# Moving three pieces of block-end work in a fused FFT and mixture-of-experts kernel

## The chip, the cores and the metric

The kernel runs on one core of one Trainium2 chip. The metric is the device time of one execution in microseconds (us). Engines are named TensorE (PE in the profile; its weight loads are PEld), VectorE (DVE), ScalarE (ACT), GpSimd (POOL) and SyncE (SP, which issues most DMAs).

## The reference

```python
X = np.fft.fft(np.fft.fft(x, axis=1), axis=2).real       # x: (8, 3072, 256), then (24576, 256) tokens
h = X @ w_in                                             # 256 -> 2048
x = (h * (1 / (1 + np.exp(-1.702 * h)))) @ w_out         # gelu by sigmoid, 2048 -> 256
# second layer, on tokens with x @ w_skip > 0; the others stay as they are
e_idx = np.argmax(x @ w_gate, axis=1)                    # 8 experts
y = gate_w * (np.maximum(x @ w1[e_idx], 0) @ w2[e_idx])  # 256 -> 1024 -> 256, weighted by the softmax
out = x + y
```

## The kernel before

Phase 1 (`Phase1`) does the transform and the first layer and sends each token's row to its expert's region in DRAM; phase 2 (`Phase2`) runs the experts. The change is in phase 1.

The sequence transform uses symmetries, so each of the 8 batches is two half-batches ("even" and "odd") of three blocks; a block makes 512 tokens. There are 48 blocks of 8 steps, 384 steps `g` in all, and the order of all instructions on each engine's queue is written out by hand. In a step:

- `hstep(g)`: twelve matmuls of 256 columns on TensorE (line 795), then on VectorE the sums `pp`, `h+`, `h-` (L799, L801, L802).
- `ystep(g - 2)`: the second product of the step before last, 24 matmuls of 264 columns (L826). It needs `gh`, and for its last third `gl`, of that step. The four results `y0` to `y3` collect in four PSUM banks over the 8 steps of a block.
- `gelu(g)`: two gelus on ScalarE (L809, L810), giving `gh` and the full value, and on GpSimd the difference `gl` (L811).
- At the end of a block, `finish`: `y0` and `y1` are copied to `rows` by VectorE, `y2` and `y3` by ScalarE (L832). The next block's product writes the same banks.
- Then the entries of `side` for this step.

`side` holds, among others: the routing of a block, one part a step: `a1` in the step behind the block's end (L836, then `route1`, L724 to L729, which ends in the one-hot matrix `oh`), `a2` (`route2`, sums over tokens on TensorE, L738 and L740), `a3` (`route3`, which adds the running base, L750 to L754), and four scatters of rows by GpSimd (L758). Further the transform of the next half-batch: `p0` runs one piece on TensorE (`piece_mm`, L252, nine matmuls), and in the next step's `side` it is evacuated by `evac_even` (L264 to L271) or `evac_odd0` and `evac_odd1` (L276 to L286). Last, in even half-batches and the first steps of odd ones, the folds of the next batch's input on VectorE (L205 to L237).

Pieces and routing sums share one PSUM bank, tag `misc`; whoever comes next waits until the last reader is done. The rows tiles are a pair of buffers (`rows`, bufs=2), which the mini tokens (8 tokens, one a batch) share. Left-over work of the loop's last blocks prepares phase 2.

Of the kernel before, what the change touches and what calls it, by code (L numbers as in the profile page):

```python
# [12 lines left out]
F32 = mybir.dt.float32  # L13
# [5 lines left out]
ALU = mybir.AluOpType  # L19
# [4 lines left out]
P = 128  # L24
# [12 lines left out]
NSTEP = NF // 2  # L37
RW = 266
NW = 264
BIG = float(1 << 20)  # L40
LAG = 2
# [115 lines left out]
class Phase1:  # L157
    def __init__(self, tc, ctx, nb, a, reg, k):
        self.tc, self.nc, self.nb, self.a, self.reg, self.k = tc, tc.nc, nb, a, reg, k
        self.ident, self.xs = k["ident"], k["xs"]  # L160
        self.side = defaultdict(list)
        self.pos = defaultdict(list)
        self.rts = {}
        self.scattered = False
        nc = self.nc
        cp = self.cp = ctx.enter_context(tc.tile_pool(name="cp", bufs=1))
        self.wch = cp.tile([P, 2, FF], F32R, name="wch")
        self.wcl = cp.tile([P, 2, FF], F32R, name="wcl")
        self.woh = cp.tile([P, NF, NW], F32R, name="woh")
        self.wol = cp.tile([P, NF, NW], F32R, name="wol")  # L170
        self.w128 = cp.tile([P, NF], F32, name="w128")
        self.coef = cp.tile([P, 2, CW], F32, name="coef")
        self.spec = cp.tile([P, 4, nb], F32, name="spec")
        self.mini = cp.tile([P, 8], F32, name="mini")
        self.tri = cp.tile([P, 2, P], BF16, name="tri")
        self.rid = cp.tile([P, 2, 4, 2], F32, name="rid")
        self.k8 = cp.tile([P, 4, 8], F32, name="k8")
        self.base = cp.tile([P, 8], F32, name="base")
        self.base0 = cp.tile([P, 8], F32, name="base0")
        dp = self.dp = ctx.enter_context(tc.tile_pool(name="dp", bufs=1, space=DRAM))  # L180
        self.yd = dp.tile([nb, 2, HC], F32, name="yd")
        self.ydm = dp.tile([nb, 1], F32, name="ydm")
        self.ps = ctx.enter_context(tc.tile_pool(name="ps", bufs=1, space=PSUM))
        self.left = ctx.enter_context(ExitStack())
        self.right = ctx.enter_context(ExitStack())
        self.yr = self.open(self.right, "yr", "right")
        self.fa = self.open(self.right, "fa", "right")
# [431 lines left out]
    def plan(self, hb):  # L619
        nc = self.nc  # L620
        b, odd = hb // 2, hb % 2
        g0 = hb * NBLK * NSTEP
        last = hb == 2 * self.nb - 1
        if last:
            return
        add = lambda s, f: self.side[g0 + s].append(f)
        le = nc.gpsimd
        st = {}
        if not odd:
# [8 lines left out]
            def p0(p):  # L638
                sh, sl = self.s
                q = self.piece_mm(st["cm"][4 + p % 2], sh, sl, p, KC)  # L640
                st["q"] = q
            def e0(p):
                st["xp"] = self.evac_odd0(b, p, st["q"])
            def e1(p):
                self.evac_odd1(p, st["xp"], st["q"], *st["y"], le)
            for p, s in enumerate((10, 13, 15, 21) if hb == 0 else (1, 4, 6, 7)):
                add(s, lambda p=p: p0(p))
                add(s + 1, (lambda p=p: e0(p)) if p % 2 == 0 else (lambda p=p: e1(p)))
            if b + 1 < self.nb:
                def ld(i):  # L650
                    st["r", i] = self.load_raw(b + 1, i // 2, i % 2)
# [36 lines left out]
        else:  # L688
# [16 lines left out]
                self.evac_even(b + 1, p, st["q"], *st["y"], le)  # L705
            for p, s in enumerate((17, 18, 20, 21) if b == 0 else (10, 13, 15, 18)):
                add(s, lambda p=p: p0(p))
                add(s + 1, lambda p=p: e0(p))
            def sp(c):
                if c == 0:  # L710
                    self.s = self.new_s()
# [28 lines left out]
            mm(ps[:, 8 * (i + 1) : n + 8], lhsT=self.tri[:, 1], rhs=o[:, : n - 8 * i], start=False, stop=i == nt - 1, skip_group_check=True)  # L740
        return ps

    def route3(self, rows, oh, ps, nt):
        nc, bp = self.nc, self.bp
        v = nc.vector
        q = bp.tile([P, 4, 8], F32, tag="rq", name="rq")
        m = bp.tile([P, 4], F32, tag="rm", name="rm")
        ix = bp.tile([P, 4], I32, tag="rix", bufs=2, name="rix")
        pv = ps[:, : nt * 8].rearrange("p (t e) -> p t e", t=nt)
        v.tensor_tensor(q[:, :nt], pv, self.base.unsqueeze(1).to_broadcast([P, nt, 8]), ALU.add)  # L750
        v.tensor_tensor(q[:, :nt], q[:, :nt], oh[:, :nt], ALU.mult)
        v.tensor_reduce(m[:, :nt], q[:, :nt], AX.X, ALU.add)
        v.tensor_scalar_add(ix[:, :nt], m[:, :nt], BIG)
        v.tensor_add(self.base, self.base, ps[:, nt * 8 : nt * 8 + 8])  # L754
        return ix

    def scatter(self, rows, ix, t):
# [14 lines left out]
    def main(self):  # L772
        nc, tc, nb = self.nc, self.tc, self.nb
        v = nc.vector
        ps = self.ps
# [6 lines left out]
        bp = self.bp  # L782
        if True:
# [30 lines left out]
            def ystep(g):  # L814
                gh, gl = gs.pop(g)
                s = g % NSTEP
                gb = g // NSTEP
                if s == 0:
                    ys[gb] = [ps.tile([P, NW], F32, tag=f"y{t}", name=f"py{t}") for t in range(4)]
                hi = [(gh, self.woh, 0), (gh, self.wol, 0), (gh, self.woh, 1), (gh, self.wol, 1)]  # L820
                lo = [(gl, self.woh, 0), (gl, self.woh, 1)]
                ends = s == NSTEP - 1
                for t, part in [(t, p_) for t in range(4) for p_ in (hi, lo)] if ends else [(t, p_) for p_ in (hi, lo) for t in range(4)]:
                    tk = slice(t * P, (t + 1) * P)
                    for n, (x_, w_, i) in enumerate(part):
                        nc.tensor.matmul(ys[gb][t], lhsT=x_[:, i, tk], rhs=w_[:, 2 * s + i], start=s == 0 and part is hi and n == 0, stop=ends and part is lo and n == 1)  # L826

            def finish(gb, gnow):
                st = {}
                rows = self.rp.tile([P, 4, RW], F32, tag="rows", bufs=2, name="rows")  # L830
                for t in range(4):
                    (v.tensor_copy if t < 2 else nc.scalar.copy)(rows[:, t, :NW], ys[gb][t])  # L832
                del ys[gb]

                def a1():
                    v.scalar_tensor_tensor(rows[:, :, NW:], self.rid[:, 1], float(gb * TB), self.rid[:, 0], ALU.mult, ALU.add)  # L836
                    st["oh"] = self.route1(rows, 4)
                    nc.sync.dma_start(self.a["out"][gb * TB : (gb + 1) * TB].rearrange("(t p) d -> p t d", p=P), rows[:, :, :D])

                def a2():  # L840
                    st["ps"] = self.route2(st["oh"], 4)

                def a3():
                    st["ix"] = self.route3(rows, st["oh"], st["ps"], 4)

                left = nhb * NBLK - 1 - gb
                if left == 0:
                    self.last_block(a1, a2, a3, lambda t: self.scatter(rows, st["ix"], t))
                    return
                for i, f in enumerate((a1, a2, a3)):  # L850
                    self.side[gnow + 1 + i].append(f)
                for t in range(4):
                    self.side[gnow + 4 + (t // 2 if left == 1 else t)].append(lambda t=t: self.scatter(rows, st["ix"], t))
                if left == 1:
                    self.side[gnow + 5].append(pad0)
                if left == 2:
                    self.side[gnow + 8].append(self.ahead_load)
# [17 lines left out]
            g = 0  # L875
            while g < total + LAG or any(k >= g for k in self.side):
                pos = lambda k: [f() for f in self.pos.pop((g, k), [])]
                pos("a")
                if g < total:
                    hstep(g)  # L880
                pos("b")
                pos("c")
                done = 0 <= g - LAG < total
                if done:
                    ystep(g - LAG)
                if g < total:
                    gelu(g)
                    if g % NSTEP == (6 if g < NSTEP else 2) and g // NSTEP + 1 < nhb * NBLK:
                        self.load_r(g // NSTEP + 1)
                if done and (g - LAG) % NSTEP == NSTEP - 1:  # L890
                    finish((g - LAG) // NSTEP, g)
                pos("d")
                for f in self.side.pop(g, []):
                    f()
                g += 1


    def plan_mini(self, g0):
        nc, bp, nb = self.nc, self.bp, self.nb
        v = nc.vector  # L900
        st = {}
# [29 lines left out]
                    nc.tensor.matmul(py[:nb], lhsT=x_[:, f], rhs=w_[:, f], start=f == 0 and n == 0, stop=f == NF - 1 and n == 2)  # L931

        def rows():
            r = st["rows"] = self.rp.tile([P, 4, RW], F32, tag="rows", bufs=2, name="rows")
            v.memset(r[:, 0], 0.0)
            v.tensor_copy(r[:nb, 0, :NW], st["py"][:nb])

# [7 lines left out]
            st["ps"] = self.route2(st["oh"], 1)  # L945

        def a3():
            st["ix"] = self.route3(st["rows"], st["oh"], st["ps"], 1)

        def sc():  # L950
            self.scatter(st["rows"], st["ix"], 0)
# [371 lines left out]
```

## Time and profile before

| | |
|---|---|
| median of 3 runs | 2459.79 us (2459.58 to 2465.42) |
| profiled execution | 2456.81 us, its span 2455.0 us |
| TensorE busy | 2374.6 us (97%) |
| VectorE busy | 1674.5 us (68%) |
| GpSimd busy | 1412.2 us (58%) |
| ScalarE busy | 1120.3 us (46%) |
| mean granted TensorE clock | 0.987 |

The step loop runs from about 38 to 1900 us. A usual step takes 4.3 us, one with a piece of the transform 5.9. In the rows, a line gives the start, the duration, engine, source line, operation, out<-in, shapes, a count, and in brackets the idle time of the engine before it and what ended it. Matmul records overlap, since matmuls are pipelined.

### The profile page before, as it was taken

What the parts mean: (1) busy time and instruction counts of PE and PEld (TensorE: products, weight loads), DVE (VectorE), ACT (ScalarE), POOL (GpSimd) and SP (SyncE); (2) the same over time, 40 slices, a digit from 0 to 9 for tenths busy, and PEclk for the clock granted to TensorE, in tenths of its full rate; (3) what the DMA queues carried; (4) which work ended last, traced back from release to release, by engine and by line L of the source; (5) the groups of instructions that cost most, each with busy time, mean ns of one, the idle gap of its engine ahead of it and who ended that gap; (6) DMA issues with size and microseconds to landing.
All of it is one profiled execution on the core that took longest, in us unless ns stands there. A gap on an engine that the chain in (4) does not pass through costs nothing. (4 is left out here: it accounts for less than half of the span.)

```text
span 2455.0 us, 50694 instructions
## 1 busy us (share of the span) xinstructions
PE 2374.6 (97%) x19222; PEld 2338.1 (95%) x19222; DVE 1674.5 (68%) x3454; ACT 1120.3 (46%) x1451; POOL 1412.2 (58%) x875
## 2 busy tenths in 40 slices
PE   5999999999999999999999999999999999999999
PEld 3799999999999999999999999999999899999998
DVE  8779669857966886698579668865656444545443
ACT  4645445454454554554544554545445233433332
POOL 4467666776766766767767767667656212323211
PEclk8999999999999999999999999999999999999999
DMA  7212211231222113112312221130100312323111
GB/s 249 96 58 74 96 55 45 85 104 42 77 67 90 47 58 121 37 45 85 104 42 77 72 84 47 58 103 21 64 23 28 105 50 79 109 83 120 36 44 35
DMA packets 91450, 178.82 MB, mean 73 GB/s; under 512 B 10895, under 2 KB 66750, under 8 KB 85104
## 3 DMA queue, kind: packets, MB, share of 16 engines
q1 hardware_dynamic: 70800, 98.21, 13.1%
q0 software_dynamic: 20448, 77.87, 9.2%
q8 instruction: 132, 2.16, 0.4%
q14 instruction: 70, 0.57, 0.1%
HBM read 126.21 MB, written 66.59 MB: 79 GB/s over the span
## 5 line engine op out<-in xcount | busy, mean ns | idle before, releaser
L811 POOL TENSOR_TENSOR gl<-h,gh 128x1024 fp32r<-128x1024 f32 x384 | 923.5, 2405 | 534.1 <-ACT h L810 453.0
L809 ACT ACTIVATE gh<-h 128x1024 fp32r<-128x1024 f32 x384 | 407.5, 1061 | 869.8 <-DVE h L802 733.3
L826 PE MATMUL py<-woh,gh 128*128 128x264 f32 x3072 | 776.8, 286 | 11.4 <-ACT rows L832 9.1
L826 PE MATMUL py<-wol,gh 128*128 128x264 f32 x3072 | 773.0, 285 | 0.0
L826 PEld LDWEIGHTS py<-woh,gh 128*128 128x128 f32 x3072 | 580.8, 189 | 16.2 <-ACT rows L832 15.6
L826 PEld LDWEIGHTS py<-wol,gh 128*128 128x128 f32 x3072 | 581.6, 189 | 0.0
L799 DVE SCALAR_TENSOR_TENSOR pp<-rb,w,pt 128x256 f32<-128x256 f32 x768 | 333.3, 475 | 337.7 <-PE pt L795 337.0
L826 PE MATMUL py<-woh,gl 128*128 128x264 f32 x3072 | 460.8, 285 | 0.7 <-POOL gl L811 0.7
L795 PE MATMUL pt<-yh,wch 128*128 128x256 f32 x1536 | 436.3, 284 | 4.3 <-ACT w L450 2.0
L795 PE MATMUL pt<-yl,wch 128*128 128x256 f32 x1536 | 432.4, 281 | 1.1 <-POOL yl L266 0.7
L795 PE MATMUL pt<-yh,wcl 128*128 128x256 f32 x1536 | 431.6, 281 | 0.0
L810 ACT ACTIVATE h<-h 128x1024 f32<-128x1024 f32 x384 | 407.4, 1061 | 35.9 <-ACT gh L809 0.7
L826 PEld LDWEIGHTS py<-woh,gl 128*128 128x128 f32 x3072 | 409.0, 189 | 1.8 <-POOL gl L811 1.4
L801 DVE TENSOR_TENSOR h<-pp,pt 128x512 f32<-128x512 f32 x384 | 263.9, 687 | 54.5 <-POOL gl L811 3.8
L795 PEld LDWEIGHTS pt<-yh,wch 128*128 128x128 f32 x1536 | 291.3, 190 | 5.3 <-ACT yh L265 2.3
L795 PEld LDWEIGHTS pt<-yl,wch 128*128 128x128 f32 x1536 | 290.7, 189 | 1.5 <-POOL yl L266 0.9
L795 PEld LDWEIGHTS pt<-yh,wcl 128*128 128x128 f32 x1536 | 290.5, 189 | 0.0
L1203 POOL DMA_INDIRECT out<-ob,ix x82 | 80.4, 980 | 355.0 <-DVE ob L1217 352.8
L802 DVE TENSOR_TENSOR h<-pp,pt 128x512 f32<-128x512 f32 x384 | 261.0, 680 | 0.0
L758 POOL DMA_INDIRECT xs<-rows,rix x193 | 193.5, 1003 | 45.0 <-issue 26.7
L1191 PE MATMUL h<-xh,w1h 128*128 128x256 f32 x656 | 188.6, 287 | 17.6 <-PEq L1253 15.3
L1225 PE MATMUL po<-w2h,hh 128*128 128x256 f32 x656 | 189.8, 289 | 0.0
(211 smaller groups left out, 3536.4 us busy)
## 6 DMA issues: line engine op xcount, KB each, us to landing
cmat<-cm POOLq DMA_DIRECT2D x48, 1158.0 KB, 5.6
raw<-raw SPq DMA_DIRECT2D x48, 512.0 KB, 5.0
out<-rows SPq DMA_DIRECT2D x48, 512.0 KB, 2.9
r<-w SPq DMA_DIRECT2D x16, 1024.0 KB, 6.6
nx<-xs SPq DMA_DIRECT2D x33, 266.0 KB, 3.0
rb<-yd SPq DMA_DIRECT2D x48, 128.0 KB, 3.3
wide<-w_in SPq DMA_DIRECT2D x8, 512.0 KB, 3.8
wide<-w_out SPq DMA_DIRECT2D x8, 512.0 KB, 5.3
```

The lines of the kernel that those rows point to most:

```text
L758: i = self.nc.gpsimd.indirect_dma_start(self.xs, bass.IndirectOffsetOnAxis(ap=ix[:, t : t + 1], axis=0), rows[:, t], None, bounds_check=E ...
L795: nc.tensor.matmul(pt[z][:, i], lhsT=w_[:, z, f], rhs=x_[:, z, cols], start=n == 0, stop=n == 2)
L799: v.scalar_tensor_tensor(pp[:, i], r, self.w128[:, 2 * s + i : 2 * s + i + 1], pt[0][:, i], ALU.mult, ALU.add)
L801: v.tensor_add(h[:, :, 0], pp, pt[1])
L802: v.tensor_sub(h[:, :, 1], pp, pt[1])
L809: nc.scalar.activation(gh, hv, AF.Gelu_apprx_sigmoid)
L810: nc.scalar.activation(hv, hv, AF.Gelu_apprx_sigmoid)
L811: nc.gpsimd.tensor_sub(gl, hv, gh)
L826: nc.tensor.matmul(ys[gb][t], lhsT=x_[:, i, tk], rhs=w_[:, 2 * s + i], start=s == 0 and part is hi and n == 0, stop=ends and part is lo an ...
L1191: nc.tensor.matmul(h[:, z], lhsT=w_[:, k, f * P : (f + 1) * P], rhs=x_[:, k], start=i == 0, stop=i == 5)
L1203: d = self.nc.gpsimd.indirect_dma_start(self.out, bass.IndirectOffsetOnAxis(ap=ix, axis=0), ob, None, bounds_check=self.ntok - 1, oob_is_e ...
L1225: self.nc.tensor.matmul(po[t], lhsT=x_[:, f, t * P : (t + 1) * P], rhs=w_[:, f], start=f == 0 and n == 0, stop=f == 7 and n == 2)
```

## The change

A second list, `pre`, is run at the head of a step, before `hstep`. The evacuations of transform pieces move from `side` to `pre` of the same step. `route3` is cut in two: its two instructions that read PSUM (adding the base to the sums, and advancing the base) go to `pre` of the step, the other three stay in `side` as `route4`. The row copies (`take`) run behind `ystep` and in front of `gelu`, where they ran behind it. The mini tokens' rows get a tile of their own.

```diff
-                add(s + 1, (lambda p=p: e0(p)) if p % 2 == 0 else (lambda p=p: e1(p)))
+                before(s + 1, (lambda p=p: e0(p)) if p % 2 == 0 else (lambda p=p: e1(p)))
...
-                add(s + 1, lambda p=p: e0(p))
+                before(s + 1, lambda p=p: e0(p))
...
-    def route3(self, rows, oh, ps, nt):
+    def route3(self, ps, nt):
+        v = self.nc.vector
+        q = self.bp.tile([P, 4, 8], F32, tag="rs", name="rs")
+        pv = ps[:, : nt * 8].rearrange("p (t e) -> p t e", t=nt)
+        v.tensor_tensor(q[:, :nt], pv, self.base.unsqueeze(1).to_broadcast([P, nt, 8]), ALU.add)
+        v.tensor_add(self.base, self.base, ps[:, nt * 8 : nt * 8 + 8])
+        return q
+
+    def route4(self, q, oh, nt):
         nc, bp = self.nc, self.bp
         v = nc.vector
-        q = bp.tile([P, 4, 8], F32, tag="rq", name="rq")
         m = bp.tile([P, 4], F32, tag="rm", name="rm")
         ix = bp.tile([P, 4], I32, tag="rix", bufs=2, name="rix")
-        pv = ps[:, : nt * 8].rearrange("p (t e) -> p t e", t=nt)
-        v.tensor_tensor(q[:, :nt], pv, self.base.unsqueeze(1).to_broadcast([P, nt, 8]), ALU.add)
         v.tensor_tensor(q[:, :nt], q[:, :nt], oh[:, :nt], ALU.mult)
         v.tensor_reduce(m[:, :nt], q[:, :nt], AX.X, ALU.add)
         v.tensor_scalar_add(ix[:, :nt], m[:, :nt], BIG)
-        v.tensor_add(self.base, self.base, ps[:, nt * 8 : nt * 8 + 8])
         return ix
...
-                for i, f in enumerate((a1, a2, a3)):
+                for i, f in enumerate((a1, a2, a4)):
                     self.side[gnow + 1 + i].append(f)
+                self.pre[gnow + 3].append(a3)
...
                 pos("a")
+                for f in self.pre.pop(g, []):
+                    f()
                 if g < total:
                     hstep(g)
...
                 if done:
                     ystep(g - LAG)
+                if ends:
+                    rows = take((g - LAG) // NSTEP)
                 if g < total:
                     gelu(g)
...
-            r = st["rows"] = self.rp.tile([P, 4, RW], F32, tag="rows", bufs=2, name="rows")
+            r = st["rows"] = self.rp.tile([P, 1, RW], F32, name="rowsm")
```

## Rows read from the trace of the kernel before

**Rows 1.** The waits of TensorE over the whole span: who waited for whom, us in total, times, longest.

```profile
PE py L826 <- ACT rows L832: 9.1, 14, 0.9
PE py L826 <- DVE rows L832: 2.1, 1, 2.1
PE pmisc L738 <- DVE yl L271: 2.0, 1, 2.0
PE pmisc L252 <- DVE yl L271: 2.0, 1, 2.0
PE pmisc L738 <- DVE xt L264: 1.4, 6, 0.2
```

**Rows 2.** Timeline from 1079 to 1087 us, the end of block 25 (in a stretch with folds) and the step behind it.

```profile
1079.09 0.28 PE L826 MATMUL py<-wol,gh 128*128 128x264 f32 x1
...
1079.81 0.64 ACT L832 COPY rows<-py 128x264 f32<-128x264 f32 x2
...
1080.22 0.39 PE L826 MATMUL py<-woh,gh 128*128 128x264 f32 x1 [0.84 <-ACT rows L832]
...
1085.70 0.19 DVE L729 TENSOR_TENSOR roh<-rq,rm 128x32 bf16<-128x32 f32 x1
...
1086.56 0.19 PE L738 MATMUL pmisc<-roh,tri 128*128 128x32 bf16 x1
```

**Rows 3.** Timeline at 1122 us: the routing of block 26, the next one.

```profile
1122.06 0.19 DVE L729 TENSOR_TENSOR roh<-rq,rm 128x32 bf16<-128x32 f32 x1
...
1122.39 0.19 PE L738 MATMUL pmisc<-roh,tri 128*128 128x32 bf16 x1
```

**Rows 4.** Busy time by stretch: the stretch, its length, then busy us (and instructions) of PE, PEld, DVE, ACT and POOL, the granted clock, the DMA share and GB/s. The first stretch has folds, the last has none.

```profile
1046.00:1140.00 94.00, 92.74 (x776) 92.02 (x775) 89.07 (x172) 46.69 (x50) 64.27 (x35) 1.00 0.18 59
...
1200.00:1268.00 68.00, 68.00 (x555) 67.95 (x555) 43.11 (x91) 34.85 (x40) 49.21 (x28) 1.00 0.14 41
```

**Rows 5.** Timeline of TensorE at 966 and at 974 us: the first product behind block 22, and the routing sums two steps later, in a later odd half-batch.

```profile
966.07 0.28 PE L826 MATMUL py<-wol,gh 128*128 128x264 f32 x1
966.36 0.39 PE L826 MATMUL py<-woh,gh 128*128 128x264 f32 x1
...
973.72 0.78 PE L826 MATMUL py<-woh,gl 128*128 128x264 f32 x5
974.73 0.18 PE L738 MATMUL pmisc<-roh,tri 128*128 128x32 bf16 x1 [0.23 <-DVE xt L264]
```

**Rows 6.** Timeline at 288 to 303 us, in the first odd half-batch: the routing sums of one step and a transform piece two steps later, with the subtraction that the first waits for.

```profile
287.59 0.53 PE L826 MATMUL py<-woh,gl 128*128 128x264 f32 x3
289.52 0.56 DVE L271 TENSOR_TENSOR yl<-pmisc,yh 128x384 fp32r<-128x384 f32 x1 [2.70 <-ACT yh L270]
290.13 0.18 PE L738 MATMUL pmisc<-roh,tri 128*128 128x32 bf16 x1 [2.01 <-DVE yl L271]
...
299.97 0.89 PE L826 MATMUL py<-woh,gl 128*128 128x264 f32 x6
302.85 0.63 PE L252 MATMUL pmisc<-cmat,sh 128*128 128x384 f32 x2 [2.00 <-DVE yl L271]
```

**Rows 7.** Timeline at 336 to 339 us: a transform piece in the second even half-batch, and the last instruction of the routing.

```profile
336.03 0.78 PE L826 MATMUL py<-woh,gl 128*128 128x264 f32 x5
...
338.99 0.16 DVE L754 TENSOR_TENSOR base<-base,pmisc 128x8 f32<-128x8 f32 x1
339.25 0.59 PE L252 MATMUL pmisc<-cmat,sh 128*128 128x384 f32 x2 [2.45 <-issue]
```

**Rows 8.** Busy time of the stretch right behind that, with columns as in rows 4.

```profile
339.60:346.00 6.40, 6.40 (x39) 6.40 (x38) 2.69 (x6) 0.60 (x2) 2.37 (x1) 0.73 0.00 0
```

**Rows 9.** Timeline at 1837 to 1839 us: the end of block 45, behind the mini tokens.

```profile
1836.63 0.28 PE L795 MATMUL pt<-yh,wcl 128*128 128x256 f32 x1
...
1838.48 0.77 DVE L832 COPY rows<-py 128x264 f32<-128x264 f32 x2 [4.30 <-DMA xs<-rows,rix]
...
1839.06 0.36 PE L826 MATMUL py<-woh,gh 128*128 128x264 f32 x1 [2.14 <-DVE rows L832]
```

**Rows 10.** Timeline at 1041 to 1056 us: the end of block 24 and its routing.

```profile
1041.01 1.06 ACT L809 ACTIVATE gh<-h 128x1024 fp32r<-128x1024 f32 x1 [1.39 <-DVE h L802]
...
1041.78 0.41 PE L826 MATMUL py<-woh,gl 128*128 128x264 f32 x2
...
1043.12 0.64 ACT L832 COPY rows<-py 128x264 f32<-128x264 f32 x2
...
1044.37 2.43 POOL L811 TENSOR_TENSOR gl<-h,gh 128x1024 fp32r<-128x1024 f32 x1
...
1045.13 1.70 DVE L836 SCALAR_TENSOR_TENSOR rows<-rid 128x8 f32<-128x8 f32 x1
...
1047.54 2.40 POOL L811 TENSOR_TENSOR gl<-h,gh 128x1024 fp32r<-128x1024 f32 x1 [0.75 <-ACT h L810]
1047.83 2.13 DVE L728 SCALAR_TENSOR_TENSOR rm<-rows,rm 128x4 f32<-128x4 f32 x1
...
1050.00 0.19 DVE L729 TENSOR_TENSOR roh<-rq,rm 128x32 bf16<-128x32 f32 x1
...
1050.67 0.19 PE L738 MATMUL pmisc<-roh,tri 128*128 128x32 bf16 x1
...
1056.12 1.10 DVE L751 TENSOR_TENSOR rq<-rq,roh 128x32 f32<-128x32 f32 x1
```

More of the change, by code (lines that the diff above doesn't have):

```diff
@@ L162, in __init__ @@
         self.pos = defaultdict(list)
+        self.pre = defaultdict(list)
         self.rts = {}
@@ L626, in plan @@
         add = lambda s, f: self.side[g0 + s].append(f)
+        before = lambda s, f: self.pre[g0 + s].append(f)
         le = nc.gpsimd
@@ L826, in ystep, with take @@
                         nc.tensor.matmul(ys[gb][t], lhsT=x_[:, i, tk], rhs=w_[:, 2 * s + i], start=s == 0 and part is hi and n == 0, stop=ends and part is lo and n == 1)
-            def finish(gb, gnow):
-                st = {}
+            def take(gb):
                 rows = self.rp.tile([P, 4, RW], F32, tag="rows", bufs=2, name="rows")
@@ L833, in finish @@
                 del ys[gb]
+                return rows
+            def finish(gb, gnow, rows):
+                st = {}
                 def a1():
@@ L843, in a3, with a4 @@
                 def a3():
-                    st["ix"] = self.route3(rows, st["oh"], st["ps"], 4)
+                    st["q"] = self.route3(st["ps"], 4)
+                def a4():
+                    st["ix"] = self.route4(st["q"], st["oh"], 4)
                 left = nhb * NBLK - 1 - gb
                 if left == 0:
-                    self.last_block(a1, a2, a3, lambda t: self.scatter(rows, st["ix"], t))
+                    self.last_block(a1, a2, lambda: [a3(), a4()], lambda t: self.scatter(rows, st["ix"], t))
                     return
-                for i, f in enumerate((a1, a2, a3)):
+                for i, f in enumerate((a1, a2, a4)):
                     self.side[gnow + 1 + i].append(f)
+                self.pre[gnow + 3].append(a3)
                 for t in range(4):
@@ L883, in main @@
                 done = 0 <= g - LAG < total
+                ends = done and (g - LAG) % NSTEP == NSTEP - 1
                 if done:
                     ystep(g - LAG)
+                if ends:
+                    rows = take((g - LAG) // NSTEP)
                 if g < total:
@@ L889, in main @@
                         self.load_r(g // NSTEP + 1)
-                if done and (g - LAG) % NSTEP == NSTEP - 1:
-                    finish((g - LAG) // NSTEP, g)
+                if ends:
+                    finish((g - LAG) // NSTEP, g, rows)
                 pos("d")
@@ L947, in a3 @@
         def a3():
-            st["ix"] = self.route3(st["rows"], st["oh"], st["ps"], 1)
+            st["ix"] = self.route4(self.route3(st["ps"], 1), st["oh"], 1)
         def sc():
```

## The prediction

> **What bounds the kernel now.** The forecast rests on three readings. First the waits of TensorE over the whole span, to see which of its waits the diff touches at all. TensorE is busy 97% of the span, so in the step loop only its idle time can be won. Five kinds of wait are touched [rows 1]: the first product of a new block waiting for the row copies (14 times on ScalarE's, once on VectorE's), and the routing sums or a transform waiting until an evacuation or the base addition has left the one `misc` PSUM bank. The reader is to see that all of them together are under 20 us of 2455.
>
> Second, the timeline around each wait, because the idle time listed is too small. A matmul record lasts 0.28 us, but such matmuls start 0.12 apart. In [rows 2] the starts are 1079.09 and 1080.22: 1.13, less 0.12, is 1.01 lost, and with the slow restart (the record of 0.39) about 1.1, where the idle column says 0.84. So a wait costs its idle time and some 0.27 more, and a wait under 0.16 is not listed at all: in [rows 5] the starts 966.07 and 966.36 hide one.
>
> Third, the busy time by stretch, to see who is the bound where the stall stands. From 1046 to 1140 VectorE is busy 89.07 of 94 us, against 43.11 of 68 in a stretch without folds [rows 4]. In the folding stretch of each batch VectorE trails TensorE and never catches up until its end. A TensorE stall there is TensorE waiting for a VectorE that is late anyway; taking one gate away lets TensorE run only to the next.
>
> **The change part by part.** No instruction is removed or added in a block; they change places on VectorE, ScalarE and GpSimd. The mini tokens get a tile of 266 floats of their own, and two of the 49 rounds of routing (last block, mini tokens) keep both halves together. SP's queue keeps its order: the output DMA of a block is still issued in the step behind its copies, and the load of the correction row stays where it was. GpSimd's subtractions of transform pieces move with their evacuation in front of the step's `gl` subtraction; they read a copy that ScalarE makes early in the step, while GpSimd waits for the gelu.
>
> (a) *Own buffer for the mini rows.* The copies of block 45 wait for the scatter DMA of an earlier block's rows, since the mini rows took a buffer of the pair; VectorE sits 4.30 us and TensorE's start slips from 1836.63 to 1839.06 [rows 9]. With the own tile, block 45 gets the buffer of block 43, whose scatters ended a block before. 2.43 less 0.12, and 0.1 of restart: **2.4**. Lower bound zero, if VectorE is late there for another reason; the idle time of 4.30 excludes most of that.
>
> (b) *Evacuations in front of the sums, first odd half-batch.* The routing sums of one step and a transform of another wait for the copy to `yl`, which waits for ScalarE's cast, queued behind both gelus [rows 6]. From the last gl product (three start 0.12 apart from 287.59, so the last at 287.83) to 290.13 is 2.30, less 0.12: 2.18. The other: 300.57 to 302.85, 2.16. After the change cast and subtraction run as soon as the piece is done, while VectorE waits for the step's first product: it idled over 2 us there (2.70 in front of the very subtraction). Together **4.35**. If the cover were gone, 0.5 us more in front of the sums, with gelu output needed two steps later.
>
> (c) *Base addition in front of the sums.* In the step at 332 the transform waits until 338.99, when the last instruction of the routing frees the bank [rows 7]. The last product begins at 336.51, the transform at 339.25: 2.73, less 0.12, is 2.6. [...] The two instructions then start some 3 us earlier, as VectorE reaches the step's sums.
>
> (d) *Six later odd half-batches.* Each loses about 0.27 at the first product and, from the last gl product (974.20) to 974.73, 0.41 at the routing sums behind the evacuation to `xt` [rows 5]. VectorE is not saturated there. 6 x 0.68: **4.1**, lower bound zero if VectorE's routing is late instead.
>
> (e) *The 14 row-copy waits.* Idle 9.1 in [rows 1], with 0.27 each 12.9. These stand in seven folding stretches, two a stretch. This is where I differ from what the listing offers. With the copies in front of the gelu, the wait at 1080.22 goes, and TensorE comes 1.1 us earlier to the next step's routing sums. Those need the one-hot matrix, which VectorE finishes at 1085.70 + 0.19 = 1085.89, and they began at 1086.56 [rows 2]: slack 0.67. VectorE's chain up to there runs without a wait for TensorE, so it stays; 0.45 of the 1.1 comes back as a new wait. In the next block the slack is 1122.39 less 1122.25, 0.14 [rows 3]. From a fixed VectorE, TensorE has won at that point no more than the last slack: 0.14 for a stretch, 7 x 0.14: **1.0**. Upper bound the whole 12.9, if VectorE's chain moves up too.
>
> What moves that chain, both ways: the copies hold the gelu back. In the block of [rows 10] the last products begin at 1041.78 and the record ends 1042.19; a copy (two take 0.64) and the two gelus (2.2 together, from 1.06 each and the gaps) behind that, `gl` begins at about 1044.85, not 1044.37, and ends 0.5 later. VectorE's L836 was held until `gl` ended (1.70 us for eight elements a partition), so it is released at about 1047.3; the next `gl` still starts at 1047.54 and then catches the second or third routing instruction instead of L728 (2.13). The one-hot would come some 0.55 later. Against that, the two base instructions (0.3 with their issue) now hide in the time for which L751 is held anyway (1.10), twice in a stretch. I take zero for the sum, with -0.6 and +0.6 for a stretch as bounds.
>
> The sum: 2.4 + 4.35 + 4.2 + 4.1 + 1.0 = 16.05. The profiled execution took 2456.81 (span 2455.0 and 1.8 around it), so 2440.8; the median of the runs is 2459.79, 3.0 above it, so **2443.7**.
>
> **The rivals.** *All stalls go.* VectorE's chain moves with TensorE. For it speaks that many of its long instructions are held and only occasionally long; against it the busy share in [rows 4]. Then 12.9 in place of 1.0: 2459.8 - 28 = 2431.8.
>
> *The early evacuations do not free TensorE.* Cast and subtraction still wait behind a late gelu, or the clock falls elsewhere, and (b) and (c) give a third: 8.55 becomes 2.9 and the time 2449.4. Against it speaks VectorE's idle time in [rows 6].
>
> *The late gelu catches the routing once more (the other side).* Only the 18 block ends with slacks under 0.7 matter ([rows 2, 3, 10] show one of each kind). If `gl` holds one more routing instruction in the first of them, the whole 2.4 goes into VectorE's chain, and six stretches lose 2.4 less 0.14 each, 13.6: 2459.8 - 15.05 + 13.6 = 2458.3, no change. If the second block is caught too, another 6 x 2.4 makes it 2472.7, slower. It becomes slower than before by over 0.3% from 3.75 us a stretch on (22.5 in all), so from two additional holds. For it: the distances are 0.1 to 0.5 us. Against: what `gl` holds now is one instruction at a time, and holding an earlier one frees a later one.
>
> [...]
>
> **How the numbers follow.** Chances: forecast 0.58 (own range 2437 to 2449), all stalls go 0.17, early evacuations fail 0.12, the gelu's catch 0.13. About 0.3% (7.4 us) is what a measurement here tells from no change, so "faster" ends at 2452.4. Faster: 0.58 + 0.17 + nearly half of the third, 0.05: 0.80. The rest of the third, and half of the fourth, are no change: 0.14. Slower: 0.06. The range 2430 to 2453 takes the first, the third, and the part of the second (about 0.1) that leaves some of its stalls; the fourth stays out.
>
> **What would show it.** Right: the waits on rows at L832 gone from TensorE's list and new ones at the routing sums for the one-hot matrix (L729's successor), about 0.5 us, 12 to 14 times; no wait for `yl`, `xt` or the transform in the stretches of [rows 6, 7]; no DMA wait in front of the copies of block 45. Wrong: a loop shorter by over 25 us with VectorE's busy share in the folding stretch up, or routing instructions of over 2 us more often than now.

## The result, and the profile after

The changed kernel is slower: 2479.07 us median (2472.52 to 2481.36) beside 2459.68 for the kernel before on the same chip, a ratio of 1.0067 [1.0048, 1.0086], or 19.4 us. The forecast was 16.05 us the other way. The profiled execution took 2472.52 us, its span 2470.7.

The busy time of each engine over the span, and two stretches with their granted clock (columns as in rows 4 and 8). The first begins right behind the transform piece of [rows 7], which starts at 330.35 here:

```profile
PE 2374.7 (96%) x19222; PEld 2333.6 (94%) x19222; DVE 1796.0 (73%) x3454; ACT 1130.3 (46%) x1451; POOL 1414.9 (57%) x875
330.70:337.10 6.40, 6.40 (x52) 6.40 (x52) 3.08 (x6) 3.21 (x4) 4.27 (x2) 1.00 0.01 3
1046.00:1140.00 94.00, 90.23 (x749) 88.88 (x748) 89.53 (x169) 44.80 (x47) 61.47 (x33) 1.00 0.17 56
```

TensorE and GpSimd do what they did; VectorE is busy 121.5 us longer (1674.5 before) with the same 3454 instructions. In the folding stretch of [rows 4] it is as full as before, but TensorE gets fewer matmuls through (749 for 776).

The waits of TensorE over the whole span, the answer to [rows 1] (who waited for whom, us in total, times, longest):

```profile
PE pt L801 <- DVE pp L805: 15.7, 17, 2.2
PE py L832 <- POOL gl L817: 12.3, 13, 2.7
PE pmisc L740 <- DVE roh L731: 6.5, 14, 0.5
PE py L832 <- DVE rows L837: 0.5, 1, 0.5
```

The five kinds of [rows 1] are gone but for 0.5 us. Three others stand in their place: for VectorE's first sum, for GpSimd's `gl`, and for the one-hot matrix (L731 is L729 before). Over the whole span TensorE is idle 96.0 us (2470.7 less 2374.7) where it was idle 80.4, so 15.6 of the 15.7 us between the two profiled executions are idle time; the mean granted clock is as before (0.989 for 0.987). So the time went into waits of TensorE, and the question is what made VectorE late.

VectorE's groups by line show it (busy us, mean ns of one, idle before), first before, then after, for the same five routing operations and one instruction of the folds:

```profile
L836 DVE SCALAR_TENSOR_TENSOR rows<-rid 128x8 f32<-128x8 f32 x48 | 63.7, 1328 | 0.0
L725 DVE TENSOR_TENSOR rq<-rows,rm 128x32 f32<-128x32 f32 x48 | 22.7, 473 | 1.7
L726 DVE SCALAR_TENSOR_TENSOR rq<-rq,k 128x32 f32<-128x32 f32 x48 | 25.9, 540 | 1.6
L728 DVE SCALAR_TENSOR_TENSOR rm<-rows,rm 128x4 f32<-128x4 f32 x48 | 33.8, 705 | 1.7
L751 DVE TENSOR_TENSOR rq<-rq,roh 128x32 f32<-128x32 f32 x48 | 32.5, 678 | 1.7
L224 DVE TENSOR_TENSOR va<-eo 64x128 f32<-64x128 f32 x16 | 5.6, 350 | 0.2
```

```profile
L845 DVE SCALAR_TENSOR_TENSOR rows<-rid 128x8 f32<-128x8 f32 x48 | 87.3, 1819 | 0.0
L727 DVE TENSOR_TENSOR rq<-rows,rm 128x32 f32<-128x32 f32 x48 | 55.2, 1151 | 1.6
L728 DVE SCALAR_TENSOR_TENSOR rq<-rq,k 128x32 f32<-128x32 f32 x48 | 40.9, 852 | 1.6
L730 DVE SCALAR_TENSOR_TENSOR rm<-rows,rm 128x4 f32<-128x4 f32 x48 | 13.6, 283 | 1.7
L758 DVE TENSOR_TENSOR rs<-rs,roh 128x32 f32<-128x32 f32 x48 | 69.1, 1439 | 0.0
L225 DVE TENSOR_TENSOR va<-eo 64x128 f32<-64x128 f32 x16 | 18.4, 1152 | 0.2
```

Undisturbed, the routing instructions take 0.16 to 0.19 us. One of them went down (L728 before, L730 after: 20.2 us less); the other five groups rose by 120.5 us together. In what follows, a VectorE instruction is called held if it is recorded over 0.25 us longer than the fastest of its kind (same line, tiles and shape). Counted over all VectorE instructions of the step loop, without the set-up's, such holds made about 235 us in some 205 instructions before, and make about 353 us in 240 now; some 225 of the 240 end with a `gl` or within 0.6 us behind it.

The timeline at the place of [rows 10], the end of block 24 after the change (columns as there):

```profile
1043.04 2.40 POOL L817 TENSOR_TENSOR gl<-h,gh 128x1024 fp32r<-128x1024 f32 x1 [2.04 <-ACT h L816]
1043.38 2.10 DVE L845 SCALAR_TENSOR_TENSOR rows<-rid 128x8 f32<-128x8 f32 x1
...
1045.57 0.19 DVE L726 TENSOR_REDUCE rm<-rows 128x4 f32<-128x32 f32 x1
...
1045.79 2.40 POOL L817 TENSOR_TENSOR gl<-h,gh 128x1024 fp32r<-128x1024 f32 x1 [0.34 <-DVE rm L726]
1045.79 2.44 DVE L727 TENSOR_TENSOR rq<-rows,rm 128x32 f32<-128x32 f32 x1
...
1048.91 0.19 DVE L731 TENSOR_TENSOR roh<-rq,rm 128x32 bf16<-128x32 f32 x1
...
1049.15 0.18 PE L740 MATMUL pmisc<-roh,tri 128*128 128x32 bf16 x1
```

The row numbers now wait 2.10 us (1.70 before) and the next `gl` catches L727 from its first moment, 2.44 us, where it caught L728 for 2.13. From the first routing instruction to the end of the one-hot matrix it takes 5.72 us (1043.38 to 1049.10) where it took 5.06: 0.66 later, against 0.55 forecast. At this block end all is as the prediction had it: all work here runs 1.8 us earlier than before, so its `gl` at "about 1044.85" and its release of L836 "at about 1047.3" are the 1043.04 and 1045.48 above. The slack of 0.48 there (1050.19 to 1050.67) is 0.05 now.

And a place that the prediction did not look at, the folds after block 25, before and after:

```profile
1097.75 0.29 DVE L224 TENSOR_TENSOR va<-eo 64x128 f32<-64x128 f32 x1
...
1098.00 2.41 POOL L811 TENSOR_TENSOR gl<-h,gh 128x1024 fp32r<-128x1024 f32 x1 [1.51 <-ACT h L810]
```

```profile
1097.15 2.40 POOL L817 TENSOR_TENSOR gl<-h,gh 128x1024 fp32r<-128x1024 f32 x1 [1.15 <-ACT h L816]
1097.27 2.43 DVE L225 TENSOR_TENSOR va<-eo 64x128 f32<-64x128 f32 x1
...
1099.71 0.87 DVE L805 SCALAR_TENSOR_TENSOR pp<-rb,w,pt 128x256 f32<-128x256 f32 x2
...
1100.63 0.39 PE L801 MATMUL pt<-yh,wch 128*128 128x256 f32 x1 [1.45 <-DVE pp L805]
```

Before, the last fold of the step began 0.25 us ahead of `gl` and took 0.29. Now `gl` begins 0.12 ahead of it; the fold takes 2.43, the next step's sum is late by that, and TensorE stands for 1.45 us. Six of the 16 L225 are held so, one in each of six folding stretches; before, none of them was.

### The profile page after: what moved, and what is told of

Its sections match the earlier page's. It is cut to its first block, busy times and chain, and to the rows that moved or that the text cites. A ratio compares the mean times of both kernels' runs of the same rounds, so it can differ in the third digit from the quotient of the medians.

```text
span 2470.7 us, 50676 instructions
## 1 busy us (share of the span) xinstructions
PE 2374.7 (96%) x19222; PEld 2333.6 (94%) x19222; DVE 1796.0 (73%) x3454; ACT 1130.3 (46%) x1451; POOL 1414.9 (57%) x875
## 5 line engine op out<-in xcount | busy, mean ns | idle before, releaser
L832 PE MATMUL py<-woh,gl 128*128 128x264 f32 x3072 | 461.9, 285 | 12.6 <-POOL gl L817 12.3
L801 PE MATMUL pt<-yh,wch 128*128 128x256 f32 x1536 | 437.4, 285 | 20.5 <-DVE pp L805 15.7
```

The source lines that it names most:

```text
L801: nc.tensor.matmul(pt[z][:, i], lhsT=w_[:, z, f], rhs=x_[:, z, cols], start=n == 0, stop=n == 2)
```

## The experiments

**Each part alone.** Four kernels, each with one part of the diff shown in front. The copies:

```diff
+                if ends:
+                    rows = take((g - LAG) // NSTEP)
                 if g < total:
                     gelu(g)
...
-                if done and (g - LAG) % NSTEP == NSTEP - 1:
-                    finish((g - LAG) // NSTEP, g)
+                if ends:
+                    finish((g - LAG) // NSTEP, g, rows)
```

> Only the row copies move in front of the gelu. Theory C (the copies hold back the gelu, so GpSimd's gl subtraction lands on the routing behind a block's end and holds VectorE's two-input instructions): slower than before by 8 to 20 us; L836's group goes from 63.7 us busy to some 87, the two-input routing instructions L725 and L726 from 49 to some 95 together, and TensorE's new waits are for pp, gl and the one-hot matrix. Theory S (the split of the base addition does the harm): 2 to 6 us faster, since the 9 us of waits on ScalarE's row copies go and nothing takes their place, VectorE's busy time within 10 us of before (1674.5).

2486.87 us, a ratio of 1.0118 [1.0103, 1.0133] to 2458.18: 28.7 slower. Of TensorE's waits:

```profile
PE pmisc L738 <- DVE xt L264: 12.0, 12, 1.0
PE pmisc L738 <- DVE roh L729: 5.7, 13, 0.5
PE py L826 <- POOL gl L811: 5.7, 7, 2.2
```

The waits for ScalarE's copies are gone, as intended, and the row numbers (83.2 us busy) and L725 and L726 (98.4 together) rose as theory C had it. The loss is larger than its 8 to 20 us, because the largest new wait is one that it did not name. It stands in the odd half-batches and was 1.4 us in 6 [rows 1]. There the evacuation to `xt` comes behind the step's sums, and these behind the routing. Measured against TensorE's products the one-hot matrix is now 0.75 us later: the routing starts 0.25 later, and its two holds are longer (1.63 and 2.19 us before). At the place of [rows 5]:

```profile
976.28 2.08 DVE L839 SCALAR_TENSOR_TENSOR rows<-rid 128x8 f32<-128x8 f32 x1
...
978.91 2.27 DVE L726 SCALAR_TENSOR_TENSOR rq<-rq,k 128x32 f32<-128x32 f32 x1
```

Waits are not the whole of the loss. In the profiled execution the span grew by 29.4 us: TensorE's idle time by 18.3, and its busy time by 11.1, with the same number of matmuls. The granted clock is 0.91 between 1800 and 1900 us, where the kernel before has 0.97.

The evacuations alone (`add` to `before`, as in the diff in front):

> Only the evacuations of transform pieces move in front of the sums. Both theories: the waits for yl and xt go (4.35 us at 288 to 303 us, and 0.4 in each of six odd half-batches, with the 0.27 at the row copies there), so 6 to 9 us faster, VectorE's busy time about as before. A third theory E (the early subtractions of GpSimd do the harm, because they now run beside VectorE's work): slower by 5 to 15 us, VectorE's busy time up by 50 us or more.

2440.21 us, 0.9925 [0.9911, 0.9939]: 18 us faster, where the prediction's terms (b) and (d) were 8.45. VectorE is busy 1606.7 us, 67.8 less, where no theory expected a change. More than half of the time of ScalarE's copy waits went without the copies being touched:

```profile
PE py L828 <- ACT rows L834: 3.9, 7, 0.9
```

9.1 in 14 before [rows 1]. So these waits did not come from the copies' place alone; with `gl` left out (below) there is none, and the copies stand where they stood.

The base addition alone (`route3` cut in two, its head in `pre`):

> Only the base addition is split off and runs in front of the sums. Theory S (the masked multiplication L751 now starts right behind h-, and meets one gl, the index conversion L753 the next): slower by 5 to 15 us, those two groups from 49 us busy to about 110. Theory C: 3 to 5 us faster, since the transform at 336 us no longer waits (2.6 us and the clock behind it), the two groups within 10 us of before.

2473.43 us, 1.0062 [1.0049, 1.0075]: 15.2 slower, at the edge of what theory S expected, but not by its mechanism: the two groups that it named rose from 48.6 us to 54.1 only. Its own stall, 339 us in [rows 7], is gone; the fold of the timeline above is caught as there (L225 18.5 us in 16 for 5.6), and TensorE has

```profile
PE pt L800 <- DVE pp L804: 7.7, 13, 0.8
PE py L831 <- POOL gl L816: 5.0, 7, 0.8
```

that it had once each before. The profiled execution (2466.06 us) was the fastest of the five.

The mini tokens' own tile alone:

> Only the mini rows get a tile of their own. All theories: the DMA wait in front of the copies of block 45 goes, 2.4 us faster (2 to 3), and nothing else changes in the profile.

2457.49 us, 0.9998 [0.9988, 1.0008]: no difference that can be measured, where 2 to 3 us were expected. The DMA wait is gone, and TensorE wins 2.3 us in block 45. It loses 2.0 of them again in the next two blocks: a VectorE instruction of the left-over work meets a `gl`, the step's sum comes late, and TensorE waits 1.91 us for it.

```profile
1852.99 2.47 DVE L1141 TENSOR_TENSOR w2l<-r,w2h 128x512 fp32r<-128x512 f32 x1 [2.85 <-ACT w2h L1140]
```

**Together, without one.** The parts do not add: 28.7 - 18.0 + 15.2 - 0.7 is 25.2, and the whole is 19.4. So the whole change was also run without its copies and without its base addition.

> The changed kernel with the row copies back behind the gelu; the rest of the change stays. If the copies are the main harm: 2459 less 18 (evacuations) plus 0 to 15 (base addition): 2441 to 2456, and VectorE's busy time under 1650. If the base addition keeps its price of 15 us beside the early evacuations, 2452 to 2458; if its price was that of one fold instruction caught by a gl in each folding stretch, which other shifts undo, 2436 to 2446.

2449.58 us, 0.9960 [0.9947, 0.9973]: faster than before.

> The changed kernel without the split of the base addition: copies, evacuations and mini tile. If parts add: 2459 + 28.7 - 18 - 1 = 2469. If copies are harmful only where VectorE is late, which the early evacuations partly cure: 2450 to 2465, the group of L836's successor still over 70 us busy.

2462.27 us, 1.0011 [1.0000, 1.0023]. Against the whole change the copies cost 1.07%, the base addition 0.56%. With evacuations and mini tile alone:

> The two parts that did not cost anything alone: evacuations in front of the sums, and the own tile of the mini rows. If parts add: 2458 less 18 and less 0.7 to 2.4, 2437 to 2440. If holds depend on small shifts all over: anywhere within 10 us of 2440.

2443.50 us, 0.9917 [0.9901, 0.9932]: 18.2 us faster. These two parts alone give about what was forecast for the whole, though not by the forecast's sum (below).

**Shorter pieces of gl.** If VectorE waits for the rest of a GpSimd instruction, two halves should hold it for less.

```diff
-                nc.gpsimd.tensor_sub(gl, hv, gh)
+                for i in range(2):
+                    nc.gpsimd.tensor_sub(gl[:, i], hv[:, i], gh[:, i])
```

In the changed kernel:

> The changed kernel, with each gl subtraction of GpSimd (128x1024, 2.4 us) made as two of 128x512. Theory H (VectorE's instructions with two SBUF inputs are held until the GpSimd instruction in progress ends): no hold is longer than some 1.2 us; the mean of L845's group falls from 1819 ns to under 1300, VectorE's busy time from 1796 to under 1720, and the time from 2479 to 2435 to 2462. A rival (VectorE is late for another reason, its instructions are merely recorded long): VectorE's busy time within 20 us of 1796, the time within 8 us of 2479 or slower, since GpSimd issues 384 more instructions.

2470.33 us, 1.0028 [1.0017, 1.0040]: better than the whole change (1.0067), but less than theory H asked for, in the time as in VectorE's busy time (1748.2 us). Held instructions became shorter and more: about 308 us in some 325 (353 in 240). The row numbers came down (52.9 us for 87.3), while the one-hot matrix, which no `gl` had reached before, is now caught:

```profile
L731 DVE TENSOR_TENSOR roh<-rq,rm 128x32 bf16<-128x32 f32 x48 | 42.9, 894 | 1.6
```

On top of evacuations and mini tile:

> The same with the gl subtraction in two halves. Theory H: the holds halve, the last row-copy waits (seven, 3.9 us idle) stay or shrink, 2425 to 2437. The rival: no gain, 2437 to 2445.

2440.37 us, 0.9907 [0.9892, 0.9922], not to be told from 0.9917; the expectation of a gain missed. VectorE is even busier (1637.0 us for 1610.0), and here too the one-hot matrix is caught now (24.7 us for 9.2). Half the length did not halve the cost in either kernel; that the second half catches what comes next is the author's reading, which was not shown by itself.

**Without gl.** The question left open by the halves was whether the holds are the cause or merely stand beside it. Four kernels leave the `gl` subtraction out; the second product reads `gh` in its place, so they compute something else, with every other instruction kept.

```diff
-                nc.gpsimd.tensor_sub(gl, hv, gh)
-                gs[g] = (gh, gl)
+                gs[g] = (gh, gh)
```

> The kernel before, with GpSimd's gl subtraction left out: the last third of the second product reads gh in gl's place, so it computes something else (about twice the first layer's output); all matmuls, gelus, sums, copies and routing instructions stay. Both theories: VectorE's instructions are no longer held (its busy time falls by 150 us or more from 1674.5), and the time falls by 10 to 40 us, to 2420 to 2450, since VectorE no longer trails in the folding stretches. It is the base for the next three.

The kernel before, so cut: 2428.69 us (2427.85 to 2431.41), 31.9 less than with `gl`. VectorE is busy 1447.2 us, 227.3 less, with the same instructions.

> The whole change, with the gl subtraction left out in the same way. Theory of the holds: the change is then the gain that was forecast or less, 5 to 16 us below the run before it, since nothing is left to be caught. Rival (the pieces cost in themselves: a gelu that starts later, two instructions more in front of the step's sums): 10 to 20 us above the run before it, as with gl.

The whole change, so cut: 2420.38 us (2418.24 to 2421.22), 8.3 less than the run before it. The page and the same routing lines:

```profile
PE 2360.8 (98%) x19222; PEld 2330.5 (96%) x19222; DVE 1450.0 (60%) x3454; ACT 1130.3 (47%) x1451; POOL 493.4 (20%) x491
L727 DVE TENSOR_TENSOR rq<-rows,rm 128x32 f32<-128x32 f32 x48 | 9.2, 192 | 1.7
L843 DVE SCALAR_TENSOR_TENSOR rows<-rid 128x8 f32<-128x8 f32 x48 | 7.7, 161 | 0.0
```

> The row copies in front of the gelu alone, with the gl subtraction left out. Theory of the holds: 0 to 13 us below the kernel before without gl (the 14 waits for ScalarE's copies go). Rival: some 20 to 29 us above it, as with gl.

2428.73 us (2425.14 to 2430.18): with 28.7 lost where `gl` runs, nothing lost here, and nothing won, since the kernel without `gl` has no wait for ScalarE's copies left to remove.

> The base addition in front of the sums alone, with the gl subtraction left out. Theory of the holds: 0 to 5 us below the kernel before without gl (the transform that waits for the base addition at 336 us starts earlier). Rival: some 10 to 15 us above it, as with gl.

2430.15 us (2429.49 to 2431.07): 1.5 above the base, inside the intervals (0.9873 [0.9857, 0.9890] and 0.9870 [0.9853, 0.9887]), for 15.2 with `gl`. In the whole change without `gl` no VectorE instruction of the step loop is held (in each of the other three seven are, by GpSimd's subtractions of transform pieces, 4 us in all), and the change is a gain. A later gelu or two instructions more in front of the sums cost nothing in themselves; they cost by where they put VectorE's instructions beside `gl`. (Leaving `gl` out also takes TensorE's waits for `gl` away, 12.3 us in 13 in the changed kernel; these four runs don't tell the one from the other.)

**Other orders.** All four row copies on VectorE in their old place, with evacuations and mini tile, and ScalarE free for the gelus:

> Evacuations in front, own mini tile, and all four row copies on VectorE in their old place, so that no copy waits behind a gelu and no gelu behind a copy. Theory C (what harms is the gelu held back, not that the copies come early): the waits of TensorE on ScalarE's copies go as in the changed kernel, the groups of L836, L725 and L726 stay near those of the evacuations alone (46, 23 and 12 us), and the time is 2430 to 2442; VectorE gets 0.85 us more a block, which may cost up to 5 us in the folding stretches. If copies that come early are harmful as such: 2455 or more.

2441.12 us, 0.9911 [0.9895, 0.9926]. Then the row numbers written right behind the copies, a step earlier than before, where mostly no `gl` runs yet:

```diff
                     v.tensor_copy(rows[:, t, :NW], ys[gb][t])
+                v.scalar_tensor_tensor(rows[:, :, NW:], self.rid[:, 1], float(gb * TB), self.rid[:, 0], ALU.mult, ALU.add)
```

> Evacuations, mini tile, four copies on VectorE, and the row numbers (before: L836 at the head of the routing) written right behind the copies, a step earlier, where GpSimd has not yet begun the block end's gl. Theory H (a hold is set by the moment at which the instruction is issued): the group falls from 39 us busy to under 20, the rest of the routing starts up to 2 us earlier and may be caught elsewhere; 2430 to 2441. If the instruction is long by itself: no change, 2441 within 3.

2436.96 us, 0.9905 [0.9889, 0.9922], the lowest median of those that compute the whole, though its ratio is not to be told from 0.9907 and 0.9911. The group of the row numbers, and the stretch of [rows 4]:

```profile
L836 DVE SCALAR_TENSOR_TENSOR rows<-rid 128x8 f32<-128x8 f32 x48 | 10.8, 226 | 0.0
1046.00:1140.00 94.00, 94.00 (x784) 93.90 (x784) 76.96 (x173) 46.64 (x46) 70.84 (x40) 1.00 0.18 60
```

VectorE has 17 of 94 us to spare in the stretch where it had 5, with one instruction more, and TensorE no idle time there. What was read in front as VectorE's work was in good part VectorE's waiting. Last, the whole of `a1` a step earlier:

```diff
-                for i, f in enumerate((a1, a2, a3)):
-                    self.side[gnow + 1 + i].append(f)
+                a1()
+                for i, f in enumerate((a2, a3)):
+                    self.side[gnow + 2 + i].append(f)
```

> As the one before, but the whole first part of the routing (row numbers to one-hot) runs at once behind the copies, a step earlier. Theory H: the chain takes 1.3 us, and the block end's gl begins some 1 to 2 us behind the copies, so either the chain is through before it (2428 to 2438, holds of the routing's instructions under 30 us in all), or it is caught as before, and the next step's sums come late (2440 to 2455).

2568.25 us, 1.0445 [1.0430, 1.0460]: the largest loss, far outside both expectations, with the same instructions in another order (the output DMA of a block is issued a step earlier too). Now 38 of the 48 L211, a fold, are held, against 13 in the changed kernel, where the group takes 33.2 us:

```profile
PE pt L797 <- DVE pp L801: 60.1, 47, 2.2
L211 DVE TENSOR_TENSOR eo<-pq 128x256 f32<-128x256 f32 x48 | 85.4, 1779 | 1.5
```

In the profiled execution the span grew by 111.5 us: TensorE's idle time by 74.2, and its busy time by 37.3 for the same number of matmuls, at a mean granted clock of 0.976 (0.987 before).

## Why the prediction was wrong

**The bound was read as work.** [Rows 4] were taken to say that VectorE is full in a folding stretch and that its chain is fixed. It was full of holds: without `gl`, 227.3 us of its busy time go.

**Where the time went.** The second product (L826) has the same 9216 matmuls in the same order in all these kernels. The start of the first one of each block, in two traces, therefore says how far one kernel has fallen behind the other. Against the kernel before, us won (-) and lost (+) in the profiled executions, for the whole change and for three parts alone (blocks count from 0, six to a batch):

| | forecast | whole | evacuations | base addition | copies |
|---|---|---|---|---|---|
| block 5, term (b) | -4.35 | -4.6 | -4.5 | -0.1 | +3.0 |
| block 6, term (c) | -4.2 | -4.3 | -4.3 | -4.3 | 0.0 |
| six folding stretches (blocks 1 to 3 of a batch), term (e) | -0.85 | +18.5 | -5.4 | +15.8 | +3.4 |
| the six stretches between them, term (d) | -4.1 | +0.5 | -4.0 | -1.2 | +9.9 |
| blocks 43 to 47, term (a) | -2.4 | +9.3 | +0.1 | +0.4 | +13.0 |
| all the rest | -0.15 | -3.7 | +2.6 | -1.5 | +0.1 |
| span | -16.05 | +15.7 | -15.5 | +9.1 | +29.4 |

Most of the rest is the set-up and the first blocks, and says little: they took 4.4 us more in the execution with the tile alone, an edit that does not touch them.

**(a)** The DMA wait went as said, and the gain was given back in the next two blocks, as the tile alone shows. The reason that the prediction gave for a lower bound of zero, a VectorE late for something else, came true one block later than it looked. In the time it can't be seen either way: 0.9998 [0.9988, 1.0008] leaves 0.7 with 2.5 either way.

**(b), (d)** Right in mechanism and, for the evacuations alone, in size (4.5 and 4.0). The routing sums now follow the last product at once. The last `gl` products and what comes behind them in the whole change, in the two places of [rows 6]:

```profile
285.24 1.14 PE L832 MATMUL py<-woh,gl 128*128 128x264 f32 x8
286.21 0.19 PE L740 MATMUL pmisc<-roh,tri 128*128 128x32 bf16 x1
...
295.76 1.13 PE L832 MATMUL py<-woh,gl 128*128 128x264 f32 x8
296.73 0.51 PE L253 MATMUL pmisc<-cmat,sh 128*128 128x384 f32 x2
```

The evacuations gave 18.0 (15.0 to 21.9) because they also won block 6 and 5.4 us in the folding stretches. What was missed there: they change VectorE's holds, from about 235 us to 154. Of the difference, 19 us are holds by GpSimd's own subtraction of a transform piece, which moved with the evacuation (20 VectorE instructions ended with one before, one after); the rest are holds by `gl`. In the whole change the copies take (d) back.

**(c)** The wait of [rows 7] went, and the clock reads 1.00 in the stretch that answers to [rows 8], where it read 0.73. The 4.2 for this term, in the forecast's sum and in the 8.55 of the second rival, is 2.6 for the wait and 1.6 that the author put on the low clock; no run shows the 1.6 by itself. What the runs show in its place is 4.3 us won in block 6, wait and clock together. But the evacuations alone win the same 4.3, so beside them the base addition had nothing left to win. The step that failed is the last sentence of the prediction's (c), that the two instructions merely "start some 3 us earlier", at no price. With them, whatever VectorE does behind them meets `gl` at another moment: at the folds after block 25, in the run of the base addition alone, `h-` begins 0.49 us behind the start of the running `gl` where it began 0.85 behind it. In each of six folding stretches that is one caught fold more (L225, held 2.1 us too long), and TensorE loses 2.3 to 2.7 us in each, whichever other parts stand beside it; with `gl` left out, the same edit loses nothing there.

**(e)** The first half came as written: the copy waits gone and, in their place, a wait for the one-hot matrix of about 0.5 us, 14 times. The step that failed is the last one, "I take zero for the sum, with -0.6 and +0.6 for a stretch as bounds". In the whole change, against the run without the copies, they cost 1.4 to 1.8 us in each folding stretch. The 0.55 for the block of [rows 10] was about right (0.66), but one block was taken to stand for the stretch, and only block ends in folding stretches were looked at. Of the 29.4 us that the copies lose alone, 3.4 stand there, 9.9 between them (the routing sums behind `xt`) and 13.0 in the last five blocks. Those last ones, where the clock is lower too, were not traced to single instructions.

**The rival nearest to the result** is the late gelu's catch, at 0.13: slower, 2479 where it said up to 2472.7. It was priced with the right unit, a whole hold of 2.4, and the routing groups show its mechanism. Its place was only part of it: beside the evacuations and the tile, the other two parts lose 4.0 us in a folding stretch, and 2.3 to 2.7 of them are the caught fold, which the rival did not have. What spoke against it, that holding an earlier instruction frees a later one, is in the groups above: 20.2 us freed, 120.5 taken on. That it is `gl` which holds, the runs show: in the changed kernel some 225 of 240 holds end with one or within 0.6 us behind it, and in the whole change without `gl` there are none.

## What to carry to other kernels

Where GpSimd runs long instructions beside VectorE's (2.4 us here), read VectorE's mean by kind against the fastest of the kind before calling it busy; here the excess was waiting (227.3 us of VectorE's 1674.5 went with `gl`), and it moved when anything moved. An edit that shifted such instructions by a few tenths of a microsecond cost a whole GpSimd instruction here (a fold of 0.29 us took 2.43 once `gl` began 0.12 us ahead of it, where it had begun 0.25 behind it), so the bound of such an edit is that length times all the meeting places, not the shift. Here leaving the long GpSimd instruction out was worth 31.9 us (TensorE's waits for it included), twice the forecast for the listed waits; moving single short instructions out of its way was worth too little to tell. Test the parts one by one: here one part carried all the gain and two the loss. And lay the traces side by side by an instruction that both have, to see in which stretch each part won or lost.

## What was not expected of the hardware

Not only instructions with two SBUF inputs are held. The index conversion L760 of the changed kernel has one, four values a partition, and took 2.22 us in one place, 0.17 undisturbed. Here two `gl` in a row catch two instructions of one step, and between them a reduction, also of one input, goes through; below, the groups of the two over the whole span:

```profile
1203.88 4.90 POOL L817 TENSOR_TENSOR gl<-h,gh 128x1024 fp32r<-128x1024 f32 x2 [2.94 <-ACT h L816]
1203.92 2.41 DVE L758 TENSOR_TENSOR rs<-rs,roh 128x32 f32<-128x32 f32 x1
1206.37 0.19 DVE L759 TENSOR_REDUCE rm<-rs 128x4 f32<-128x32 f32 x1
...
1206.59 2.22 DVE L760 TENSOR_SCALAR rix<-rm 128x4 int32<-128x4 f32 x1
```

```profile
L760 DVE TENSOR_SCALAR rix<-rm 128x4 int32<-128x4 f32 x48 | 40.8, 849 | 1.7
L729 DVE TENSOR_REDUCE rm<-rq 128x4 f32<-128x32 f32 x48 | 8.9, 186 | 1.6
```

The reductions are never held in any of the kernels: of the changed kernel's, 12 begin inside a running `gl`, and with `gl` in halves 80, and none takes over 0.191 us. The conversion is held each time it begins inside one, 16 of 16 in the changed kernel, at 2.19 to 2.22 us each (170 ns on the mean in the kernels where it meets none). The conversion of the mini tokens, one value a partition instead of four, is not held: in the kernel before it begins 0.32 us into a `gl` and takes 155 ns. Nor is `pp` (L799 before), which has one of its inputs in PSUM: some 220 begin inside a `gl`, and all take 0.46 to 0.48 us. Theories C and H had named two-input instructions alone.
